# Tensor sums moved from GpSimd to VectorE, attention of two head groups in one operation: an attention and FFN kernel

## Chip, core and metric

The kernel runs on one core of one Trainium2 chip. The time is that of the device from launch to end, in microseconds. Of a kernel the median of several runs is given; one more execution, with the profiler on, gave the trace. TensorE is called PE in the profile (PEld is its weight load), VectorE DVE, ScalarE ACT, GpSimd POOL, SyncE SP.

## What is computed

```python
def _attn_ref(q, k, v):                     # 8 batches, 8 heads, 576 tokens, 64 columns
    chunk, scale = 64, 1.0 / np.sqrt(D)     # attention inside chunks of 64 tokens
    scores = scale * np.matmul(q_c, k_c.transpose(0, 1, 2, 4, 3))
    scores = scores - np.max(scores, axis=-1, keepdims=True)
    attn = np.exp(scores)
    attn = attn / (np.sum(attn, axis=-1, keepdims=True) + 1e-09)
    return np.matmul(attn, v_c)

def _moe_ref(x, w_in, w_out):               # x 4608 x 512, w_in 512 x 2048, w_out 2048 x 512
    h = x @ w_in
    g = np.where(h >= 1, h, np.where(h <= -1, 0.0, (h + 1) ** 2 / 4.0))
    return (g @ w_out).astype(np.float32)
```

x is the attention's result with the heads side by side. The weights come in 64-bit floats, q, k and v in 32-bit ones.

## The kernel before

**Tiles.** The 4608 tokens are nine tiles of 512: tiles 0 to 5, 7 and 8 are the first 512 tokens of a batch, tile 6 collects the last 64 of all eight. A tile has four head groups of two heads each (128 columns of x). In SBUF x stands with its columns on the partitions, so FFN1 gives h by blocks of 128 hidden columns by 512 tokens.

**Products.** Each 32-bit operand is split into a high part that PE takes in its fast 32-bit format and a low part, the rest; a product is high x high + high x low + low x high, three matmuls of 512 columns. The high part is a copy on ScalarE, the low part a subtraction on VectorE (`ffn_split` L760, `split` L1050, `parts` L946, `attn_split_banks` L723).

**Tiles 0 to 2** are done one by one: `ffn_in` makes a block of h (L739), the curve (ScalarE L746, L749; VectorE L750) makes g, `ffn_split` its parts, `ffn_out` (L774) adds the block's share to four banks of PSUM. At the tile's end `store` (L792 on VectorE, L794 on ScalarE) moves the banks into two buffers and SP sends them out. Meanwhile `mix_weights` makes, for 16 pairs of weight blocks, the sums that a seven-product scheme for 2 x 2 blocks needs: per call two sums of 512 columns on GpSimd and four of 256 columns on VectorE (L837), ScalarE's copies (L859), VectorE's low parts (L860), and DMAs from GpSimd into a DRAM tensor `mixed` (L823). SCHEDULE (L262) says at which block (tile x 16 + block) each call is added, and which buffers it uses.

**Tiles 3 to 8** are done in three pairs with seven products in place of eight. `mix_x` (L937, L944, L946) makes the combinations of x. For FFN1, `ffn_quad(t, m)` does seven products n of 1.36 us each for two blocks of hidden columns of two tiles, in the order SEQ = (1, 5, 6, 3, 7, 2, 4), into two banks (ps_h for even m, ps_o for odd m), with sums of what stands in the banks (L975, L981) and the curve (L1008 to L1012). Four quads make a half. Then `ffn_mixed_out` takes the half's 28 steps of FFN2: `split` (ScalarE L1049, VectorE L1050) and the products, with `less` (L985) making the next combinations of g. The weights of both come back from `mixed` by GpSimd's DMAs (L887, 512 KB for two products), into a ring of seven buffers; `stream(done)` asks for the next ones. The results are transposed on VectorE and sent by SP (`store_turned`, L1089, L1110, L1118).

**Attention** of the next tiles goes beside the FFN, for tiles 2 and up in bursts of two head groups: values of the current two groups (L568) and scores of the next two (L550) on PE, then for each group by itself max, subtraction, exp, sum, reciprocal and product (`attn_softmax`, L626 to L644), a transpose in 32 x 32 blocks (L675), and eight SP transfers for both groups (`move`, L668) that put the blocks in place. q and k are transposed the same way (`attn_turn`, L524). The product by the reciprocal is on GpSimd for tiles 0, 2, 3 and 4.

**Order.** Nothing is emitted directly. Every step goes to a `Plan` with an engine, a cost, what it reads and writes, and a lag from its end to its use (a DMA's landing). The plan is run twice in the kernel's build: once in the order of the program, from which due times are worked out backwards, then engine by engine, always the step that is ready and has the earliest due time. That order becomes each engine's queue, which runs in order on the chip. Steps of the kind "any" (`less` L985, the subtractions of `mix_x` L937) go to VectorE or GpSimd, whichever takes them first in the plan. `port=True` marks steps that the plan doesn't let overlap on the two engines:

```python
            if port:
                start = max(start, port_free)
            end = self.products_end(start, cost, columns) if e == "pe" else start + cost
            if port:
                port_free = end
```

Of the kernel before, what the change touches and what calls it, by code (L numbers as in the profile page):

```python
# [211 lines left out]
def kernel(  # L212
# [15 lines left out]
    nc = tc.nc  # L228
# [27 lines left out]
    PAIRED = 3  # L256
# [4 lines left out]
    OWN, RING5, EARLIER, LATER = range(4)  # L261
# [10 lines left out]
    def buffers(pool, name, n, dtype=F32):  # L272
# [73 lines left out]
    def e_room(t, g):  # L346
        return room("e", kT_bufs if t > 1 else e_bufs, t, g)
# [139 lines left out]
    def load_heads(t, g, which="qkv"):  # L487
        for n, src, bufs in (("q", q, q_bufs), ("k", k, k_bufs), ("v", v, v_bufs)):
# [5 lines left out]
            if BATCH[t] is None or (n, t) == ("v", TURNED):  # L494
# [6 lines left out]
                (), (key,), lag=2.1 if t < 3 else 4.1, moving=1.3 if load == load_blocks else 1.2,  # L501
# [15 lines left out]
    def attn_turn(t, g):  # L517
        for n, (name, bufs, src_bufs, dst_bufs) in enumerate(
# [38 lines left out]
    def values_of(t, g):  # L557
# [6 lines left out]
        def product(n, h, half):  # L564
            at = (2 * n + h) * C if t < FLIPPED else h * HALF + n * C
            of = h * HALF + n * C
            rows = slice(half * C, (half + 1) * C)
            nc.tensor.matmul(  # L568
                out=values[half][h * C:(h + 1) * C, n * C:(n + 1) * C],
                lhsT=v_sb[rows, of:of + C], rhs=aT[rows, at:at + C], start=True, stop=True,  # L570
            )
# [43 lines left out]
    def attn_softmax(t, g):  # L615
# [5 lines left out]
        e4 = e.rearrange("p (n h k) -> p h n k" if t < FLIPPED else "p (h n k) -> p h n k", h=2, k=C)  # L621
        mx4 = mx.rearrange("p (h n) x -> p h n x", h=2)
        sm4 = sm.rearrange("p (n h) x -> p h n x" if t < FLIPPED else "p (h n) x -> p h n x", h=2)
# [18 lines left out]
        on_pool = t < 1 or t in (2, 3, 4)  # L642
# [15 lines left out]
    def attn_turn_back_pair(some):  # L658


        xkeys, akeys = ([f"{n}{i}" for i in range(2)] for n in ("qT", "aT"))

        def move():
            src, dst = (x.rearrange("p g (c e q) -> p (g c) e q", e=2, q=Q) for x in (qT_both, aT_both))
# [7 lines left out]
        for t, g in some:  # L672
            ekey, e = e_room(t, g)
            xkey, x = room("x", qT_bufs, t, g)
            plan.add("dve", 0.6, lambda x=x, e=e: nc.vector.transpose(out=x, in_=e), (ekey,), (xkey,))  # L675
        plan.add("sp", 5.4, move, xkeys, akeys, lag=4.9, moving=0.8, sends=8)
# [127 lines left out]

    def step_of(w, m, n):
# [11 lines left out]
    def to_mixed(w, m, which, key, src, cols, after):  # L817
# [5 lines left out]
        plan.add("pool", 0.65, lambda: nc.gpsimd.dma_start(  # L823
            out=mixed[steps[0] // LONG][:, rows, cols], in_=src()
        ), key, [f"mixed{step}_{cols.start}" for step in steps], lag=2.1, moving=0.8, after=after)

    def mix_weights(kind, m, scratch, after):
# [44 lines left out]
    def engine_of(e):  # L872
        return nc.vector if e == "dve" else nc.gpsimd

    RING = [f"wi{j}" for j in range(6)] + ["wo0"]
    X_TAGS = [f"wi{j}" for j in range(6, NF)]
    asked_for = [0]

    def stream(done):


        while asked_for[0] < min(len(RING) + done // 2, (NTILE - PAIRED) // 2 * STEPS // 2):
            step, tag = asked_for[0] * 2 % STEPS, RING[asked_for[0] % len(RING)]
            asked_for[0] += 1
            keys = [f"mixed{n}_{at}" for n in (step, step + 1)
                    for at in ((0,) if product_of[n] in SINGLE else (0, HALF))]
            plan.add("pool", 0.65, lambda step=step, tag=tag: nc.gpsimd.dma_start(  # L887
                out=place_of(tag).bitcast(F32), in_=mixed[step // LONG][:, step % LONG:step % LONG + 2, :]
            ), keys, (f"{tag}_0", f"{tag}_1"), lag=2.1, moving=1.4)

    def streamed(t, w, m, n):


        step = (t - PAIRED) // 2 * STEPS + step_of(w, m, n)
        tag, at = RING[step // 2 % len(RING)], step % 2
        return f"{tag}_{at}", lambda: place_of(tag)[:, at, :]
# [28 lines left out]
    def mix_x(t):  # L925
# [63 lines left out]
    def ffn_quad(t, m):  # L989


        abank, bbank = h_banks if m % 2 == 0 else o_banks[:2]
        s_, w_, u_ = H_SUMS[m % 2]
        k = m % PARTS
# [11 lines left out]
        def curve(src, dst):  # L1006
            (hkey, h), (rkey, r) = src, dst
            plan.add("act", 0.5, lambda: nc.scalar.activation(  # L1008
                out=r(), in_=h(), func=AF.Relu, bias=0.5, scale=0.5
            ), (hkey,), (rkey,))  # L1010
            plan.add("act", 0.52, lambda: nc.scalar.square(out=r(), in_=r()), (), (rkey,))  # L1011
            plan.add("dve", 0.6, lambda: nc.vector.scalar_tensor_tensor(  # L1012
                out=r(), in0=h(), scalar=1.0, in1=r(), op0=ALU.max, op1=ALU.min
            ), (hkey,), (rkey,))
# [9 lines left out]
        curve(u_, X12[k])  # L1024
        products(7, bbank, False)
        total_of(w_, bbank, w_)
        curve(w_, X22[k])
        products(2, abank, True)
        total_of(s_, abank, s_)
        curve(s_, X11[k])  # L1030
        products(4, bbank, False)
        curve(whole(bbank), X21[k])
# [9 lines left out]
    def ffn_mixed_out(t, half, at):  # L1042
# [14 lines left out]
        for index, n in enumerate(SEQ):  # L1057
# [24 lines left out]
            done = (t - PAIRED) // 2 * STEPS + step_of("wo", half * PARTS + PARTS - 1, n) + 1  # L1082
            stream(done)

    def store_turned(t, n, src, ending=False):
# [3 lines left out]
        plan.add("dve", 0.6, lambda: nc.vector.transpose(out=o(), in_=x()), (key,), (okey,))  # L1089
# [30 lines left out]
        plan.add("sp", 0.6 * sends, send, (okey,), (), lag=2.3, moving=0.9, sends=sends)  # L1120
# [48 lines left out]
    def scratch_of(where):  # L1169
# [5 lines left out]
        if where == OWN:  # L1175
            return [S_BUFS[n] for n in (0, 3, 4, 0)]
        if where == EARLIER:
# [176 lines left out]
```

## Time and profile before

| | us |
|---|---|
| median of 3 runs (lowest, highest) | 854.37 (853.62, 856.25) |
| the profiled execution's own time | 856.74 |
| its span, first to last instruction | 855.0 |
| PE busy | 807.4 |
| DVE busy | 713.7 |
| ACT busy | 494.1 |
| POOL busy (DMA issues among it) | 359.9 |

Busy is the time in which at least one instruction of the engine was under way. Matmuls are pipelined, one starts before the last ends. The span's stages, by the trace: to 120 us attention of the first tiles, tile 0 and the preparation of the weights; to 236 tile 1; to 365 tile 2; to 530, 700 and 845 the three pairs; then the last store.

### The profile page before, as it was taken

The page shows a single profiled execution, that of the slowest core. Times are in us where ns is not written, and L with a number is a line of the kernel's source. Part 1 is how long each engine was busy: PE and PEld are TensorE (multiplying, and loading weights), DVE is VectorE, ACT ScalarE, POOL GpSimd, SP SyncE. Part 2 cuts the span into 40 slices and gives each one's busy share as a digit, 9 for nine tenths or more (in the row PEclk, how much of TensorE's full clock was granted, in tenths as well). Part 3 has the DMA queues.
Part 4 walks back from the last instruction along what each step waited for, and adds up shares of the span by engine and source line. Part 5 has one row for each costly group of instructions (what it writes and reads, how often), then busy time and mean ns, then how long its engine had stood idle before and what let it go on. Part 6 is the DMA issues. An engine that isn't in the chain of part 4 may idle for free.

```text
span 855.0 us, 15680 instructions
## 1 busy us (share of the span) xinstructions
PE 807.4 (94%) x5648; PEld 655.4 (77%) x5648; DVE 713.7 (83%) x1092; ACT 494.1 (58%) x870; POOL 359.9 (42%) x419
## 2 busy tenths in 40 slices
PE   9999999989989989999998799899998999999995
PEld 8888878877768868878886578778786877788873
DVE  4989986989669888999797899798589986866795
ACT  5999844534426444765476436564477456637741
POOL 1000015886656681464526353254138532631351
PEclk9999999999999999999999999999999999999998
DMA  9995758796799795998998469999774599566654
GB/s 201 279 314 112 204 113 228 221 291 190 217 214 304 177 277 123 271 243 226 262 261 210 141 184 217 224 242 262 204 203 142 168 265 250 177 193 189 191 168 79
DMA packets 334350, 180.38 MB, mean 211 GB/s; under 512 B 293824, under 2 KB 302016, under 8 KB 334272
## 3 DMA queue, kind: packets, MB, share of 16 engines
q0 software_dynamic: 33152, 117.46, 42.7%
q1 hardware_dynamic: 296896, 61.12, 35.6%
q10 hardware_dynamic: 4224, 0.79, 0.6%
q8 instruction: 45, 0.74, 0.4%
q14 instruction: 33, 0.27, 0.1%
HBM read 133.17 MB, written 38.80 MB: 201 GB/s over the span
## 4 chain that ended last, share of the span: by engine, by line
PE 49%; DVE 20%; DMA 11%; SPq 6%; issue 5%; POOL 4%; ACT 3%; DVEq 0%; POOLq 0%; ACTq 0%
PE ps_o L966 22%; PE ps_h L739 8%; PE ps_o L774 7%; PE ps_h L966 7%; DMA out_dram<-tmp 3%; DVE big_wo L1050 3%; DMA k_sb<-in_k_dram 2%; POOL mixed L823 2%; DVE gl L1050 2%; DVE big_wo L1012 2%; DMA aT_both<-qT_both 1%; PE ps_h L1314 1%; DVE big_wo L975 1%; DVE big_wi L946 1%; SPq L470 1%
## 5 line engine op out<-in xcount | busy, mean ns | idle before, releaser
L887 POOL DMA_DIRECT2D big_wi<-mixed x144 | 78.2, 544 | 198.3 <-PE ps_o L966 132.0
L739 PE MATMUL ps_h<-xh,parts_wi 128*128 128x512 f32 x376 | 128.5, 402 | 8.3 <-DVE r L750 4.4
L774 PE MATMUL ps_o<-parts_wo,gh 128*128 128x512 f32 x384 | 120.5, 395 | 4.4 <-DVE tmp L792 4.4
L966 PE MATMUL ps_o<-big_wo,big_wi 128*128 128x512 f32 x432 | 107.8, 393 | 3.6 <-DVE big_wo L1050 3.4
L966 PE MATMUL ps_o<-gh,big_wi 128*128 128x512 f32 x288 | 98.7, 396 | 7.6 <-DVE big_wo L1012 5.4
L966 PEld LDWEIGHTS ps_o<-big_wo,big_wi 128*128 128x128 f32 x432 | 80.7, 189 | 23.1 <-DVE big_wo L1050 6.4
L985 POOL TENSOR_TENSOR big_wo<-big_wo,big_wo 128x512 f32<-128x512 f32 x55 | 85.9, 1571 | 25.7 <-DVE gl L1050 15.0
L739 PEld LDWEIGHTS ps_h<-xh,parts_wi 128*128 128x128 f32 x376 | 72.6, 193 | 25.6 <-DVE r L750 5.6
L966 PE MATMUL ps_o<-big_wi,big_wi 128*128 128x512 f32 x360 | 88.1, 396 | 0.2 <-ACT big_wo L981 0.2
L966 PE MATMUL ps_h<-big_wi,big_wi 128*128 128x512 f32 x360 | 86.6, 391 | 0.0
L774 PEld LDWEIGHTS ps_o<-parts_wo,gh 128*128 128x128 f32 x384 | 71.3, 189 | 19.9 <-DVE tmp L792 5.2
L1050 DVE TENSOR_TENSOR big_wo<-big_wo,big_wo 128x512 fp32r<-128x512 f32 x84 | 79.1, 950 | 4.0 <-ACT big_wo L1049 4.0
L1049 ACT CAST big_wo<-big_wo 128x512 fp32r<-128x512 f32 x84 | 52.0, 622 | 51.9 <-PE ps_o L966 28.5
L966 PEld LDWEIGHTS ps_o<-big_wi,big_wi 128*128 128x128 f32 x360 | 67.3, 189 | 16.4 <-ACT big_wo L981 1.9
L966 PEld LDWEIGHTS ps_h<-big_wi,big_wi 128*128 128x128 f32 x360 | 68.0, 189 | 14.8 <-ACT r L981 0.5
L1050 DVE TENSOR_TENSOR gl<-big_wo,gh 128x512 fp32r<-128x512 f32 x84 | 77.3, 927 | 2.2 <-ACT gh L1049 2.0
L774 PE MATMUL ps_o<-parts_wo,gl 128*128 128x512 f32 x192 | 75.6, 394 | 0.2 <-issue 0.2
L739 PE MATMUL ps_h<-xl,parts_wi 128*128 128x512 f32 x188 | 75.0, 399 | 0.0
L1049 ACT CAST gh<-big_wo 128x512 fp32r<-128x512 f32 x84 | 52.0, 621 | 38.0 <-PE ps_o L966 32.4
L966 PEld LDWEIGHTS ps_o<-gh,big_wi 128*128 128x128 f32 x288 | 54.6, 190 | 22.2 <-DVE big_wo L1012 7.0
L975 DVE TENSOR_TENSOR big_wo<-ps_o,big_wo 128x512 f32<-128x512 f32 x84 | 55.7, 677 | 6.4 <-PE ps_o L966 6.3
L1011 ACT ACTIVATE big_wo<-big_wo 128x512 f32<-128x512 f32 x96 | 59.4, 630 | 1.9
(205 smaller groups left out, 1669.7 us busy)
## 6 DMA issues: line engine op xcount, KB each, us to landing
big_wi<-mixed POOLq DMA_DIRECT2D x144, 512.0 KB, 4.9
big_wo<-mixed POOLq DMA_DIRECT2D x24, 512.0 KB, 4.5
mixed<-tmp POOLq DMA_DIRECT2D x36, 256.0 KB, 4.3
words_wi<-in_moe_w_in_dram SPq DMA_DIRECT2D x16, 512.0 KB, 6.3
words_wo<-in_moe_w_out_dram SPq DMA_DIRECT2D x16, 512.0 KB, 6.7
aT_both<-qT_both SPq DMA_DIRECT2D x112, 64.0 KB, 3.8
v_sb<-in_v_dram SPq DMA_DIRECT2D x52, 128.0 KB, 4.2
q_sb<-in_q_dram SPq DMA_DIRECT2D x104, 64.0 KB, 4.3
```

The source lines that it names most:

```text
L470: queue.dma_start(out=dst[r:r + Q, :, e, :], in_=rows[:, e * Q:(e + 1) * Q, :].rearrange("c p d -> p c d"),)
L739: nc.tensor.matmul(out=ps, lhsT=weight["wi", j][:, half, kc * P:(kc + 1) * P], rhs=x(), start=(kc == 0 and i == 0), stop=(kc == KC - 1 and ...
L774: nc.tensor.matmul(out=acc, lhsT=x[:, cols], rhs=weight["wo", j][:, half, :], start=(j == 0 and i == 0), stop=(j == NF - 1 and i == 2),)
L823: plan.add("pool", 0.65, lambda: nc.gpsimd.dma_start(out=mixed[steps[0] // LONG][:, rows, cols], in_=src()), key, [f"mixed{step}_{cols.sta ...
L887: plan.add("pool", 0.65, lambda step=step, tag=tag: nc.gpsimd.dma_start(out=place_of(tag).bitcast(F32), in_=mixed[step // LONG][:, step % ...
L966: nc.tensor.matmul(out=bank, lhsT=w[:, part * HALF + c * P:part * HALF + (c + 1) * P], rhs=rhs, start=fresh and begin and k == 0, stop=end ...
L975: plan.add("dve", 0.6, lambda: nc.vector.tensor_tensor(out=o(), in0=b, in1=x(), op=ALU.add), (bkey, xkey), (okey,))
L985: plan.add("any", (0.6, 1.1), lambda e: engine_of(e).tensor_tensor(out=o(), in0=x(), in1=y(), op=ALU.subtract), (xkey, ykey), (okey,), por ...
L1011: plan.add("act", 0.52, lambda: nc.scalar.square(out=r(), in_=r()), (), (rkey,))
L1012: plan.add("dve", 0.6, lambda: nc.vector.scalar_tensor_tensor(out=r(), in0=h(), scalar=1.0, in1=r(), op0=ALU.max, op1=ALU.min), (hkey,), ( ...
L1049: plan.add("act", 0.52, lambda: nc.scalar.copy(out=h(), in_=x()), (key,), (hkey,))
L1050: plan.add("dve", 0.6, lambda: nc.vector.tensor_tensor(out=l(), in0=x(), in1=h().bitcast(F32), op=ALU.subtract), (key, hkey), (lkey,), por ...
```

## The change

1. The two wide sums of `mix_weights`, the subtractions of `mix_x` and all of `less` are VectorE's. GpSimd keeps DMA issues and the softmax product of tile 0.
2. From tile 2 on, attention's operations on VectorE and ScalarE take both groups of a burst at once: q, k and their transposes, the softmax and its transpose are 128 x 1024. For that the buffers of two groups are one tile (`twin`). The transposed result is first copied whole on ScalarE; then four SP transfers instead of eight put the off-diagonal blocks in place.
3. FFN1's products of neighbouring quads are interleaved in the program and in the stream's order: quad m + 1 begins after four products of quad m (PACE = 2). `stream` is called after each product instead of after each quad.
4. The plan's lags: transfers into and out of `mixed` 3.3 instead of 2.1 us, turned stores 3.3 instead of 2.3, loads of q, k, v for tile 2 4.1 instead of 2.1. Some costs in the plan are changed by a few hundredths.
5. SCHEDULE has other places and buffers for the 16 calls of `mix_weights`; the last is at 44 instead of 47.

New functions for one more way of doing tiles (`ffn_quad_held`, `recall`) are added and not called, since MIXED equals PAIRED. The diff, cut:

```diff
-    PAIRED = 3
+    PAIRED, MIXED, PACE = 3, 3, 2
...
     SCHEDULE = (
-        (17, RING5), (18, EARLIER), (18, EARLIER), (20, RING5), (22, RING5), (23, EARLIER),
-        (25, RING5), (27, RING5), (31, RING5), (34, RING5), (35, LATER), (37, RING5),
-        (37, RING5), (42, RING5), (43, OWN), (47, OWN),
+        (17, EARLIER), (18, RING5), (20, EARLIER), (20, EARLIER), (20, RING5), (22, RING5),
+        (27, RING5), (31, RING5), (32, RING5), (34, LATER), (37, RING5), (37, RING5),
+        (38, RING5), (39, OWN), (43, OWN), (44, OWN),
     )
...
-                (), (key,), lag=2.1 if t < 3 else 4.1, moving=1.3 if load == load_blocks else 1.2,
+                (), (key,), lag=2.1 if t < 2 else 4.1, moving=1.3 if load == load_blocks else 1.2,
...
+    def attn_turn_pair():
+        for src, dst in (("q_sb", "qT"), ("k_sb", "kT")):
+            plan.add("dve", 1.18, lambda src=src, dst=dst: nc.vector.transpose(
+                out=flat[dst], in_=flat[src]
+            ), [f"{src}{i}" for i in range(2)], [f"{dst}{i}" for i in range(2)])
...
-        on_pool = t < 1 or t in (2, 3, 4)
+        on_pool = t < 1
...
-    def attn_turn_back_pair(some):
+    def attn_softmax_pair():
+        keys = {n: [f"{n}{i}" for i in range(2)] for n in ("ps_a", "mx", "sm", "kT", "qT", "aT")}
+        sc = a_pair.rearrange("p h (m k) -> p (h m) k", k=C)
+        e3 = flat["kT"].rearrange("p (m k) -> p m k", k=C)
+        plan.add("dve", 1.13, lambda: nc.vector.tensor_reduce(
+            out=mx_both, in_=sc, axis=AX.X, op=ALU.max
+        ), keys["ps_a"], keys["mx"])
+        plan.add("dve", 1.13, lambda: nc.vector.tensor_tensor(
+            out=e3, in0=sc, in1=mx_both.broadcast_to([P, 2 * G, C]), op=ALU.subtract
+        ), (*keys["ps_a"], *keys["mx"]), keys["kT"])
+        plan.add("act", 0.9, lambda: nc.scalar.activation(
+            out=flat["kT"], in_=flat["kT"], func=AF.Exp, scale=SCALE
+        ), (), keys["kT"])
+        def norm():
+            nc.vector.tensor_reduce(out=sm_both, in_=e3, axis=AX.X, op=ALU.add)
+            nc.vector.tensor_scalar_add(sm_both, sm_both, 1e-9)
+            nc.vector.reciprocal(out=sm_both, in_=sm_both)
+        plan.add("dve", 1.6, norm, keys["kT"], keys["sm"])
+        plan.add("dve", 1.13, lambda: nc.vector.tensor_tensor(
+            out=e3, in0=e3, in1=sm_both.broadcast_to([P, 2 * G, C]), op=ALU.mult
+        ), keys["sm"], keys["kT"], port=True)
         def move():
...
             for j in range(2):
-                for i in range(4):
-                    a, b = ((2 * j + n) * Q for n in divmod(i, 2))
-                    nc.sync.dma_start(
-                        out=dst[b:b + Q, :, i // 2, :], in_=src[a:a + Q, :, i % 2, :]
-                    )
...
-        plan.add("sp", 5.4, move, xkeys, akeys, lag=4.9, moving=0.8, sends=8)
+                for n in range(2):
+                    a, b = (2 * j + n) * Q, (2 * j + 1 - n) * Q
+                    nc.sync.dma_start(out=dst[b:b + Q, :, n, :], in_=src[a:a + Q, :, 1 - n, :])
+        plan.add("dve", 1.18, lambda: nc.vector.transpose(out=flat["qT"], in_=flat["kT"]), keys["kT"], keys["qT"])
+        plan.add("act", 0.9, lambda: nc.scalar.copy(out=flat["aT"], in_=flat["qT"]), keys["qT"], keys["aT"])
+        plan.add("sp", 2.7, move, keys["qT"], keys["aT"], lag=4.9, moving=0.4, sends=4)
...
+    QUAD_ORDER = sorted(
+        ((m, n) for m in range(PARTS) for n in SEQ), key=lambda x: (len(SEQ) * x[0] + PACE * SEQ.index(x[1]), x[0])
+    )
+    OUT_ORDER = [(k, n) for n in SEQ for k in range(PARTS)]
...
-        at = k * len(SEQ) + SEQ.index(n) if w == "wi" else SEQ.index(n) * PARTS + k
+        at = (QUAD_ORDER if w == "wi" else OUT_ORDER).index((k, n))
...
-    STEPS = NF * len(SEQ)
+    STEPS, SLACK = NF * len(SEQ), 1.2
...
-        ), key, [f"mixed{step}_{cols.start}" for step in steps], lag=2.1, moving=0.8, after=after)
+        ), key, [f"mixed{step}_{cols.start}" for step in steps], lag=2.1 + SLACK, moving=0.8, after=after)
...
-            plan.add("pool" if wide else "dve", 1.1 if wide else 0.35, lambda: (nc.gpsimd if wide else nc.vector).tensor_tensor(
+            plan.add("dve", 0.6 if wide else 0.35, lambda: nc.vector.tensor_tensor(
...
-                plan.add("any", (0.6, 1.1), lambda e, i=i: engine_of(e).tensor_tensor(
+                plan.add("dve", 0.6, lambda i=i: nc.vector.tensor_tensor(
                     out=o()[:, i, :], in0=x()[:, i, :], in1=y()[:, i, :], op=ALU.subtract
...
-        plan.add("any", (0.6, 1.1), lambda e: engine_of(e).tensor_tensor(
+        plan.add("dve", 0.6, lambda: nc.vector.tensor_tensor(
             out=o(), in0=x(), in1=y(), op=ALU.subtract
...
-        plan.add("sp", 0.6 * sends, send, (okey,), (), lag=2.3, moving=0.9, sends=sends)
+        plan.add("sp", 0.55 * sends, send, (okey,), (), lag=3.3, moving=0.9, sends=sends)
...
-            for m in range(half * PARTS, (half + 1) * PARTS):
-                if m == 0:
-                    out_until(t * NF - 1)
-                ffn_quad(t, m)
-                stream((t - PAIRED) // 2 * STEPS + step_of("wi", m, SEQ[-1]) + 1)
-                if m in QUAD_BURSTS and more:
+            quads = [ffn_quad(t, half * PARTS + k) for k in range(PARTS)]
+            for part, n in QUAD_ORDER:
+                m = half * PARTS + part
+                quads[part](n)
+                stream(position(t, "wi", m, n) + 1)
+                if n == SEQ[-1] and m in QUAD_BURSTS and more:
```

## Rows read from the trace of the kernel before

**Rows 1.** Page: busy us (share of the span) and instructions.

```profile
PE 807.4 (94%) x5648; PEld 655.4 (77%) x5648; DVE 713.7 (83%) x1092; ACT 494.1 (58%) x870; POOL 359.9 (42%) x419
```

**Rows 2.** Table by stage: length; busy PE, PEld, DVE, ACT, POOL (count); clock; DMA; GB/s.

```profile
120.00:236.00 116.00, 110.54 (x854) 90.40 (x845) 94.43 (x159) 52.21 (x90) 80.43 (x92) 0.99 0.78 220
236.00:365.00 129.00, 121.59 (x989) 98.41 (x987) 108.61 (x173) 66.03 (x118) 72.26 (x85) 0.97 0.87 229
365.00:530.00 165.00, 154.08 (x1123) 122.85 (x1122) 148.86 (x214) 95.84 (x168) 76.36 (x88) 0.99 0.83 218
530.00:700.00 170.00, 161.84 (x985) 130.72 (x984) 145.11 (x211) 99.65 (x175) 73.59 (x84) 0.98 0.82 213
700.00:845.00 145.00, 141.61 (x614) 114.03 (x612) 112.87 (x148) 81.00 (x138) 52.37 (x63) 1.00 0.67 187
```

**Rows 3.** Waits of PE by releaser: total us, times, longest.

```profile
PE ps_o L966 <- DVE big_wo L1050: 5.5, 3, 2.1
PE ps_o L966 <- DVE big_wo L1012: 5.4, 3, 2.0
PE ps_o L774 <- DVE tmp L792: 4.4, 2, 3.1
PE ps_h L739 <- DVE r L750: 4.4, 2, 4.1
PE ps_h L739 <- DVE xl L723: 3.9, 1, 3.9
```

**Rows 4.** Timeline: DVE, GpSimd (POOL) and PE: start us, us, instruction.

```profile
183.17 1.77 DVE L760 TENSOR_TENSOR gl<-r,gh 128x512 fp32r<-128x512 f32 x1
...
186.66 1.44 DVE L837 TENSOR_TENSOR tmp<-tmp 128x256 f32<-128x256 f32 x1
...
310.65 1.28 DVE L629 TENSOR_TENSOR kT<-ps_a,mx 128x512 f32<-128x512 f32 x2
311.85 5.17 DVE L937 TENSOR_TENSOR big_xl<-big_xl,big_xl 128x512 f32<-128x512 f32 x1
...
311.43 2.55 POOL L937 TENSOR_TENSOR big_xh<-big_xl,big_xh 128x512 f32<-128x512 f32 x2
313.94 1.29 POOL L937 TENSOR_TENSOR big_xl<-big_xl,big_xl 128x512 f32<-128x512 f32 x1
315.18 1.27 POOL L837 TENSOR_TENSOR e<-parts_wo 128x512 f32<-128x512 f32 x1
...
320.01 0.50 PE L739 MATMUL ps_h<-xh,parts_wi 128*128 128x512 f32 x1 [4.13 <-DVE r L750]
```

**Rows 5.** Groups by line, DVE: busy us, mean ns | idle before.

```profile
L414 DVE TENSOR_TENSOR parts_wi<-tmp,parts_wi 128x512 fp32r<-128x512 f32 x16 | 10.9, 683 | 0.8 <-ACT parts_wi L410 0.4
...
L837 DVE TENSOR_TENSOR tmp<-e 128x256 f32<-128x256 f32 x4 | 1.7, 418 | 1.1 <-DMA out_dram<-tmp 1.1
```

**Rows 6.** Busy DVE (and POOL): L1050, L760, L1012, L946, L985, L937, L837 in turn.

```profile
0.00:855.00 855.00, 153.73 (x168) 0.99 0.79 211
...
0.00:855.00 855.00, 42.39 (x48) 0.99 0.79 211
...
0.00:855.00 855.00, 71.44 (x96) 0.99 0.79 211
...
0.00:855.00 855.00, 33.28 (x42) 0.99 0.79 211
...
0.00:855.00 855.00, 26.27 (x31) 100.56 (x65) 0.99 0.79 211
...
0.00:855.00 855.00, 9.24 (x4) 28.59 (x20) 0.99 0.79 211
...
0.00:855.00 855.00, 32.93 (x64) 43.47 (x32) 0.99 0.79 211
```

**Rows 7.** Waits of DVE for transfers: total us, times, longest.

```profile
DVE qT_both L524 <- DMA k_sb<-in_k_dram: 5.7, 2, 4.7
...
DVE tmp L792 <- DMA out_dram<-tmp: 5.0, 1, 5.0
```

More of the change, by code (lines that the diff above doesn't have):

```diff
@@ L569, in product @@
                 out=values[half][h * C:(h + 1) * C, n * C:(n + 1) * C],
-                lhsT=v_sb[rows, of:of + C], rhs=aT[rows, at:at + C], start=True, stop=True,
+                lhsT=v_sb[rows, of:of + C], rhs=(aT if t < FLIPPED else flat["aT"])[rows, at:at + C],
+                start=True, stop=True,
             )
@@ L870, in mix_weights @@
             ], slice(0, T), after)
-    def engine_of(e):
-        return nc.vector if e == "dve" else nc.gpsimd
-    RING = [f"wi{j}" for j in range(6)] + ["wo0"]
+    RINGS = [f"wi{j}" for j in range(4)], [f"wi{j}" for j in range(6)] + ["wo0"]
     X_TAGS = [f"wi{j}" for j in range(6, NF)]
     asked_for = [0]
-    def stream(done):
-        while asked_for[0] < min(len(RING) + done // 2, (NTILE - PAIRED) // 2 * STEPS // 2):
-            step, tag = asked_for[0] * 2 % STEPS, RING[asked_for[0] % len(RING)]
-            asked_for[0] += 1
[L885 to L889, printed above, removed]
+    ALONE = NF // 2 * len(SEQ) * (MIXED - PAIRED) // 2
@@ new lines, with position, steps_at, slot_of @@
+    held_steps = [step_of("wi", m, n) for m in range(NF // 2) for n in SEQ]
+    def position(t, w, m, n):
+        step = step_of(w, m, n)
+        return held_steps.index(step) if t < MIXED else ALONE + (t - MIXED) // 2 * STEPS + step
+    def steps_at(at):
+        at -= at % 2
+        if at < ALONE:
+            return sorted(held_steps[at:at + 2])
+        return [(at - ALONE) % STEPS + n for n in range(2)]
+    def slot_of(at):
+        ring = RINGS[at >= ALONE]
+        return ring[(at - ALONE * (at >= ALONE)) // 2 % len(ring)]
@@ new lines, in stream @@
+    def stream(done, without=0):
+        while asked_for[0] * 2 < ALONE + (NTILE - MIXED) // 2 * STEPS:
+            at = asked_for[0] * 2
+            late = at >= ALONE
+            begun = done - ALONE * late
+            if begun < 0 or at - ALONE * late >= 2 * (len(RINGS[late]) - without + begun // 2):
+                return
+            asked_for[0] += 1
+            steps, tag = steps_at(at), slot_of(at)
+            keys = [f"mixed{n}_{part}" for n in steps
+                    for part in ((0,) if product_of[n] in SINGLE else (0, HALF))]
+            first, last = (step % LONG for step in steps)
+            plan.add("pool", 0.65, lambda n=steps[0] // LONG, rows=slice(first, last + 1, last - first), tag=tag: (
+                nc.gpsimd.dma_start(out=place_of(tag).bitcast(F32), in_=mixed[n][:, rows, :])
+            ), keys, (f"{tag}_0", f"{tag}_1"), lag=2.1 + SLACK, moving=1.4)
@@ L1004, in products, with curve, ffn_quad_held, hold @@
             plan.add("pe", 1.362, emit, (skey, *hkeys, *lkeys), (key,), columns=6 * T)
[L1006 to L1014, printed above, removed]
+        return products
+    def curve(src, dst):
+        (hkey, h), (rkey, r) = src, dst
+        plan.add("act", 0.5, lambda: nc.scalar.activation(
+            out=r(), in_=h(), func=AF.Relu, bias=0.5, scale=0.5
+        ), (hkey,), (rkey,))
+        plan.add("act", 0.52, lambda: nc.scalar.square(out=r(), in_=r()), (), (rkey,))
+        plan.add("dve", 0.6, lambda: nc.vector.scalar_tensor_tensor(
+            out=r(), in0=h(), scalar=1.0, in1=r(), op0=ALU.max, op1=ALU.min
+        ), (hkey,), (rkey,))
+    def ffn_quad_held(t, m):
+        i, j = 2 * m, 2 * m + 1
+        abank, bbank = h_banks if m % 2 == 0 else h_banks[::-1]
+        s_, w_, u_ = HELD_SUMS
+        products = first_product(t, m)
+        def hold(j, r):
+            rkey, r = r
+            plan.add("pool", 0.65, lambda: nc.gpsimd.dma_start(out=held[j], in_=r()), (rkey,),
+                     (f"held{j}",), lag=2.1 + SLACK, moving=0.8)
         products(1, bbank, True)
@@ L1176, in scratch_of @@
             return [S_BUFS[n] for n in (0, 3, 4, 0)]
+        if where == SPARE:
+            return [(f"wi4_{n}", lambda n=n: place_of("wi4")[:, n, :].bitcast(F32)) for n in range(2)] + S_BUFS[3:]
         if where == EARLIER:
@@ L1244, in attention @@
                 if j + 2 in BURSTS:
-                    for at in then:
-                        attn_turn(*at)
+                    if m + 1 < 2 * NP:
+                        attn_turn(*then[0])
+                    else:
+                        attn_turn_pair()
                 elif m + 1 < 2 * NP:
@@ L1272 @@
             ffn_split(t, j)
-            for n, own, what in MIX_AT:
-                if n == t * NF + j:
-                    mix_weights(*what, scratch_of(own), len(plan.parts) - 1)
+            mixes_at(t * NF + j)
     stream(0)
```

123 lines of the change are left out of this document (79 added, 44 removed).

## The prediction

> **What bounds the kernel now.** I read the busy line first: PE is busy 807.4 of 855.0 us, DVE 713.7, and GpSimd does tensor work beside its DMA issues [rows 1]. The table by stage [rows 2] says where PE loses time, in two ways: idle, and at a granted clock below full. Idle is the stage's length less PE busy: 5.5 us in 120 to 236, 7.4 in 236 to 365, 10.9 in 365 to 530, 8.2 in 530 to 700, 3.4 in 700 to 845, together 35.4. The granted clock of these stages is 0.99, 0.97, 0.99, 0.98 and 1.00; (1 - clock) times length is 1.2 + 3.9 + 1.7 + 3.4 + 0 = 10.2 us, time lost to stretches at 1.2 instead of 2.4 GHz. So 45.6 us are to be had in all. The first 120 us and the end behind 845 stay out of the count: the change hardly touches them.
>
> The waits of PE say who is late: DVE ends the five costliest, 23.6 us [rows 3]. So the question is why DVE is late, though it is less busy than PE.
>
> The timeline of 310 to 320 shows it [rows 4]. Two operations that read PSUM (L629) take 1.28 us, one every 0.60. Then a 512-column subtraction, L937, starts at 311.85 and takes 5.17 us; from 311.43 on GpSimd runs four such operations back to back. PE stops for 4.13 us, for the r that stands behind L937 in DVE's queue. L760 at 183.17, with 1.77 us, and L837 at 186.66, with 1.44, are the same on a small scale; they stand in the queue ahead of the L723 that ends a 3.9 us stall [rows 3, 4]. Undisturbed, an operation of that shape takes 683 ns (L414) [rows 5]. Sums over lines say how much that is in all [rows 5, 6]: L1050 takes 153.73 us for 168 operations instead of 168 x 0.683 = 114.7, so 39.0 too many; in the same way L760 9.6, L1012 5.9, L946 4.6, L985 5.1, L937 6.5, and L837 against 418 ns for 256 columns 6.2. Together 77 us of DVE's 713.7 are spent waiting beside GpSimd.
>
> The Trainium skill, SBUF — State Buffer, Who interferes with whom, says that the port pair which both engines share is an exclusive lock, held for one instruction by whoever issues first. By that rule L937 would have stood behind one GpSimd operation, taken about 2.0 us, and the forecast gain would be some 3 us smaller. The trace shows it behind four, and decides.
>
> **The change, part by part.**
>
> *GpSimd's sums to VectorE.* 65 (L985), 20 (L937) and 32 (L837) operations leave GpSimd [rows 6]. On DVE each adds the 0.60 us of L629 [rows 4], so 117 x 0.60 = 70 us, on an engine that PE waits for. Against them stand the 77 us. DVE's load hardly changes; what goes are single operations of 1.5 to 5 us in front of what PE waits for. GpSimd keeps its DMA issues, which no longer queue behind sums, and the products of tile 0's softmax, inside the first 120 us.
>
> *Attention of two groups at once.* For 14 pairs (tiles 2 to 8) max, subtraction, sum, product and three transposes become 1024-column operations. From 418 ns at 256 columns and 683 at 512, another 512 add about 0.53 us [rows 5]; one wide operation takes 1.13 from start to start where two took 1.20. Seven of them save 0.5 us a pair, one scalar add and one reciprocal less perhaps 0.3: 0.8 x 14 = 11 us less on DVE. The 12 products of tiles 2 to 4 that come from GpSimd add 6 x 1.13 = 7. Net 4 less. But what PE needs can now stand behind 1.2 us instead of 0.7. No row shows a 1024-column f32 operation. Bounds: a gain of 4, if DVE's time were PE's, and a loss of 0.5 on PE in each of 14 pairs, 7 us. I take a loss of 4, towards that end, since PE's stalls are waits for single operations [rows 3].
>
> *Turning back.* A 1024-column ScalarE copy per pair (an estimate of 1.1 us, DVE's wide one) is new and stands ahead of 4 transfers on SP in place of 8. What it hides behind: ScalarE is 58% busy [rows 1], and the values product that needs the tile comes a burst later. I cost it at nothing; uncovered it would be 14 x 1.1 = 15 us, and a gain of as much if four fewer issues were on the path.
>
> *FFN1 products of neighbouring quads interleaved.* The same products and banks in another order, which the ring of seven stream buffers follows. The planner orders by due time and may mix quads already, so this part may do nothing at all. Bounds: the 5.4 us of L1012, FFN1's curve [rows 3], as a gain, and the same as a loss if a ring buffer is held for two quads. I take nothing, the middle.
>
> *Longer lead.* The planner counts 1.2 us more for weights through DRAM, 1.0 for turned stores, 2.0 for the loads of tile 2. Issues move ahead on GpSimd's and SP's queues past others; no byte is added. DVE stood 5.0 us for a store's landing, which PE feels at L792, 4.4, and 5.7 for k [rows 3, 7]. Bounds: those 10.7 won; or 4.7, the longest wait for k, lost where a load moved ahead crowds another. Half is taken, inside the stage sums.
>
> *Sums of weights at other places* (from 17 to 44 instead of 17 to 47). Two of them, at 31 and 32, now stand just ahead of tile 1's store, and share buffers with it: one wait like L792's, 4.4 us, more or less. I take nothing.
>
> **The sum, by stage.** From 120 to 365: the 4.1 at L750 go, and of the 3.9 at L723 what the two operations ahead of it took too long, 1.77 - 0.68 and 1.44 - 0.42, 2.1. With L792's these are the three long stalls, so I give a third of the 5.1 us of clock to each, 3.4 to these two. Of L792's 4.4 and 1.7, half: 3.0. That makes 12.6. From 365 to 700: 19.1 us idle and 5.1 of clock, in which DVE's contention and late transfers are mixed; half, 12, and no more, since DVE stays busy there (148.86 of 165 and 145.11 of 170 us) [rows 2]. From 700 to 845 half of 3.4, 1.7. Less 4 for the wide operations: 22.3 us. The profiled execution took 856.74 around its span of 855.0, and would take 834; the median of the three runs is 854.37, and 854.4 - 22.3 = 832.
>
> **Rivals.**
>
> *DVE's queue is the bound from 365 to 700.* The operations that GpSimd did stand in the same in-order queue as everything else. For it: DVE's busy share there, 90 and 85%. Against: much of that is the waiting that goes. Then only the 12.6 of 120 to 365 are won: 842.
>
> *Nearly all of it goes.* DVE's times become regular, the planner's order holds, PE doesn't stop and keeps its clock: 854.4 - 45.6 is 809, and 812 with a few short waits left. Against: transfers end some of the waits.
>
> *The stalls move.* What was late has successors that were late too (the seven-buffer ring, the two store buffers), and a wait of the same size takes the place of each: 853.
>
> *Wide operations hold up PE, and it is slower.* A wide transpose starts when q and k of both groups have landed; DVE stands still until then, as it did for 4.7 us for one k [rows 7], and everything behind it waits. It decides once each of the 14 pairs loses PE more than 26.3 / 14 = 1.9 us, 26.3 being the gain above without the wide operations' 4. At 3 us each, 42 - 26 = 16 over before: 870. Against: there are two such waits in 855 us so far, and before, the scores of both groups were one step as well. The Trainium skill, Perfetto Trace Analysis, Optimizing Scalar/DVE Operations, says that where VectorE isn't saturated but causes bubbles on other engines, breaking instructions up may complete work sooner. By it this part goes the wrong way; with DVE 83% busy and at the end of PE's waits, the trace of before meets its condition.
>
> *The change doesn't do what it says*: that is the interleaving, above, costed at nothing.
>
> **How the numbers follow.** The forecast has a chance of 0.50, DVE's queue 0.22, nearly all 0.09, stalls that move 0.07, the wide operations 0.12. Faster by over 0.3% (2.6 us, about what a measurement of this kernel can tell from no change) is below 851.8: the first three and a little of the fourth, 0.82; within it 0.06; slower 0.12. The range goes down to 812, nearly all of it; and up to 849, the first rival with 7 us lost to the wide operations. Outside are the last two cases, under 0.2.
>
> **What would show it.** L1050 near 683 ns in the mean, and no DVE operation of 512 columns over 1 us behind 120: the contention is gone. PE idle in the two stages of tiles 1 and 2 at 6 us or less in place of 12.9, at a clock of 0.99 or more: the first term is right. DVE above 95% busy from 365 to 700 and PE's waits still at L1050 and L1012: the first rival. DVE's waits for q and k above 20 us: the slower one. The forecast is wrong in its root if L1050 falls to 683 and PE's idle time does not fall.

## The result, and the profile after

The changed kernel takes 825.12 us (median of 4 runs, 824.52 to 825.72) where the kernel before took 854.11 on the same chip: a ratio of 0.9656, interval 0.9638 to 0.9674, 29 us less. In later sessions the kernel before took 842 to 858, so what follows goes by ratios of one session and by the traces.

The page's busy line of the changed kernel, to be read against [rows 1]:

```profile
PE 794.4 (96%) x5648; PEld 652.5 (79%) x5648; DVE 684.1 (83%) x1095; ACT 501.3 (61%) x870; POOL 176.1 (21%) x290
```

The span went from 855.0 to 823.6 us. PE is busy 13.0 us less with the same 5648 matmuls, and idle 18.4 us less (47.6 to 29.2). So some 40% of the gain came out of time that the page calls busy. Of the 13.0 us, 3.4 are the granted clock: ahead of the last store 20.5 us stood at 1.2 GHz before, 13.7 now, and half the difference is lost time. Another 6.9 are short stalls that the overlapping records cover: at 2.4 GHz most 512-column matmuls start 227 ns behind the one before, and 139 starts were more than 260 ns behind in the kernel before, 86 now. DVE takes 117 sums over from GpSimd, and is busy 30 us less.

The costliest groups on DVE, against [rows 5, 6] (L1050 is now L1159, L985 is L1038, L760 is L786):

```profile
L1159 DVE TENSOR_TENSOR gl<-big_wo,gh 128x512 fp32r<-128x512 f32 x84 | 56.8, 681 | 8.8 <-ACT gh L1158 8.8
L1159 DVE TENSOR_TENSOR big_wo<-big_wo,big_wo 128x512 fp32r<-128x512 f32 x84 | 56.8, 682 | 5.9 <-ACT big_wo L1158 5.7
L1038 DVE TENSOR_TENSOR big_wo<-big_wo,big_wo 128x512 f32<-128x512 f32 x72 | 48.2, 682 | 0.2
L786 DVE TENSOR_TENSOR gl<-r,gh 128x512 fp32r<-128x512 f32 x48 | 32.8, 683 | 7.8 <-ACT gh L785 7.4
...
L673 DVE TENSOR_REDUCE mx_both<-ps_a 128x16 f32<-128x1024 f32 x14 | 17.1, 1219 | 5.0 <-PE ps_a L558 5.0
```

Every mean is at the undisturbed 683 ns; the 77 us of waiting beside GpSimd are gone. The wide operations take 1.22 us, as the extrapolation had it.

The waits of PE, against [rows 3]:

```profile
PE ps_h L765 <- ACT big_xh L729: 6.0, 1, 6.0
PE ps_o L1019 <- DVE big_wo L1159: 5.7, 1, 5.7
PE ps_o L1019 <- DVE big_wo L1066: 2.6, 2, 2.1
```

Two stalls are left that matter, at 246 and 553 us. Both end at a store. Here are SP, DVE, ACT and PE at the first (timeline; SPq are SP's DMA issues):

```profile
222.92 5.79 SPq L826 DMA_DIRECT2D out_dram<-tmp  x3
229.47 2.89 SPq L698 DMA_DIRECT2D aT_both<-qT_both  x4
232.47 14.15 SPq L466 DMA_DIRECT2D k_sb_both<-in_k_dram  x8
246.66 0.49 SPq L826 DMA_DIRECT2D out_dram<-tmp  x1
...
249.03 0.43 DVE L868 TENSOR_TENSOR tmp<-tmp,e 128x256 f32<-128x256 f32 x1 [7.11 <-DMA out_dram<-tmp]
...
250.75 0.62 ACT L890 CAST tmp<-tmp 128x512 fp32r<-128x512 f32 x1 [9.55 <-DVE e L868]
251.27 0.58 ACT L729 COPY big_xh<-ps_h 128x512 f32<-128x512 f32 x1
...
251.90 0.79 PE L765 MATMUL ps_h<-xh,parts_wi 128*128 128x512 f32 x1 [5.95 <-ACT big_xh L729]
```

The last piece of tile 1's store stands on SP's queue behind four moves and eight loads of k. A sum of weights on DVE wants the store's buffer, a cast on ACT wants the sum, and the copy that frees PE's bank stands behind the cast. At 553 it is the transpose of a turned store:

```profile
557.78 0.71 DVE L1197 STREAM_TRANSPOSE tmp<-big_wo 128x512 f32<-128x512 f32 x1 [7.73 <-DMA out_dram<-tmp]
```

**By stage.** The boundaries below are counted, not read off the clock: tiles 1 and 2 begin with the 193rd and 385th of the 576 FFN1 matmuls (L739, now L765), the three pairs with the 1st, 673rd and 1345th of the 2016 of L966 (now L1019), and the rest begins with the last of them. So tile 2 begins at 217.7 us of the kernel before and the pairs at 332.6, 511.5 and 686.5, and not at the 236, 365, 530 and 700 that are given for them ahead of the prediction. Each row is one trace, in us; the other kernels are explained below. Two traces of the same kernel (after and n1, e5 and n2) differ by up to 2.4 us in a stage.

```
kernel                start   tile 1  tile 2  pair 1  pair 2  pair 3   rest    span
before                123.2    94.5   114.9   178.9   175.0   158.2   10.3    855.0
after                 122.1    88.1   111.9   164.5   173.1   154.6    9.2    823.6
e1 sums alone         124.7    88.1   116.9   170.4   166.9   156.6    9.3    832.9
e2 sums back          122.7    88.1   108.8   179.5   175.7   161.0    9.2    845.2
e7 idle sums          124.1    93.7   110.6   186.8   187.8   173.4    9.2    885.7
e8 idle fills         123.2    90.6   109.9   165.8   170.0   155.5    9.3    824.2
e4 short lead         122.0    88.3   110.6   163.3   172.0   155.6    9.2    821.0
e6 old places         122.6    88.1   117.4   164.9   170.1   154.8    9.3    827.2
e3 quads in turn      122.9    88.4   110.9   166.0   173.0   154.8    9.3    825.4
e5 narrow             122.3    88.2   102.7   168.5   167.6   154.7    9.2    813.1
n1 after again        122.2    88.1   111.3   164.5   170.7   155.0    9.2    821.0
n2 narrow again       122.4    88.2   102.3   168.6   167.1   156.2    9.3    814.0
n3 eight transfers    121.4    88.2   114.0   178.3   166.9   154.0    9.2    832.0
n4 narrow in turn     121.7    88.1   102.3   169.7   168.2   153.8    9.3    813.0
```

### The profile page after: what moved, and what is told of

It is laid out like the page before. It is cut to its first block, busy times and chain, and to the rows that moved or that the text cites. A ratio compares the mean times of both kernels' runs of the same rounds, so it can differ in the third digit from the quotient of the medians.

```text
span 823.6 us, 15371 instructions
## 1 busy us (share of the span) xinstructions
PE 794.4 (96%) x5648; PEld 652.5 (79%) x5648; DVE 684.1 (83%) x1095; ACT 501.3 (61%) x870; POOL 176.1 (21%) x290
## 4 chain that ended last, share of the span: by engine, by line
PE 68%; DVE 12%; DMA 6%; ACT 5%; issue 5%; SPq 3%; POOL 1%; DVEq 0%; ACTq 0%; POOLq 0%
PE ps_o L1019 30%; PE ps_h L765 12%; PE ps_o L800 12%; PE ps_h L1019 8%; DMA out_dram<-tmp 3%; SPq L466 2%; DVE big_wo L1066 1%; ACT big_wo L1062 1%; PE ps_a L558 1%; DVE gl L1159 1%; DVE big_wo L1159 1%; DVE big_wo L1038 1%; ACT big_wo L1065 1%; POOL mixed L854 1%; DMA k_sb_both<-in_k_dram 1%
## 5 line engine op out<-in xcount | busy, mean ns | idle before, releaser
L765 PE MATMUL ps_h<-xh,parts_wi 128*128 128x512 f32 x376 | 127.6, 399 | 6.0 <-ACT big_xh L729 6.0
L1019 PE MATMUL ps_o<-big_wo,big_wi 128*128 128x512 f32 x432 | 107.3, 393 | 5.7 <-DVE big_wo L1159 5.7
L1019 PE MATMUL ps_o<-gh,big_wi 128*128 128x512 f32 x288 | 98.1, 395 | 3.2 <-DVE big_wo L1066 2.1
L1019 PEld LDWEIGHTS ps_o<-big_wo,big_wi 128*128 128x128 f32 x432 | 81.3, 189 | 23.5 <-DVE big_wo L1159 6.5
L765 PEld LDWEIGHTS ps_h<-xh,parts_wi 128*128 128x128 f32 x376 | 71.8, 191 | 21.8 <-ACT big_xh L729 6.4
L1019 PE MATMUL ps_o<-big_wi,big_wi 128*128 128x512 f32 x324 | 81.0, 392 | 0.9 <-DVE big_wo L1066 0.5
L1019 PE MATMUL ps_h<-big_wi,big_wi 128*128 128x512 f32 x324 | 79.4, 391 | 1.1 <-DVE big_wo L1066 1.1
L765 PE MATMUL ps_h<-xl,parts_wi 128*128 128x512 f32 x188 | 74.2, 394 | 0.0
L1019 PEld LDWEIGHTS ps_o<-big_wi,big_wi 128*128 128x128 f32 x324 | 60.3, 188 | 15.5 <-ACT tmp L1034 1.7
L1019 PEld LDWEIGHTS ps_h<-big_wi,big_wi 128*128 128x128 f32 x324 | 60.3, 188 | 14.6 <-DVE big_wo L1066 1.7
L1019 PEld LDWEIGHTS ps_o<-gh,big_wi 128*128 128x128 f32 x288 | 54.9, 191 | 15.9 <-DVE big_wo L1066 2.5
L1159 DVE TENSOR_TENSOR gl<-big_wo,gh 128x512 fp32r<-128x512 f32 x84 | 56.8, 681 | 8.8 <-ACT gh L1158 8.8
L1159 DVE TENSOR_TENSOR big_wo<-big_wo,big_wo 128x512 fp32r<-128x512 f32 x84 | 56.8, 682 | 5.9 <-ACT big_wo L1158 5.7
L1019 PE MATMUL ps_o<-gl,big_wi 128*128 128x512 f32 x144 | 56.9, 395 | 0.3 <-DVE gl L1159 0.3
```

What stands on the lines that cost most here:

```text
L765: nc.tensor.matmul(out=ps, lhsT=weight["wi", j][:, half, kc * P:(kc + 1) * P], rhs=x(), start=(kc == 0 and i == 0), stop=(kc == KC - 1 and ...
L1019: nc.tensor.matmul(out=bank, lhsT=w[:, part * HALF + c * P:part * HALF + (c + 1) * P], rhs=rhs, start=fresh and begin and k == 0, stop=end ...
L1159: plan.add("dve", 0.6, lambda: nc.vector.tensor_tensor(out=l(), in0=x(), in1=h().bitcast(F32), op=ALU.subtract), (key, hkey), (lkey,), por ...
```

## Experiments

Theories: A, GpSimd's sums held up VectorE's and so PE. B, the gain comes from the lead, the places or the order of products. C, VectorE's queue is the bound. D, GpSimd's results and DMA issues came late, and its neighbourhood as such cost nothing. E, SP's queue became shorter.

**e1, the sums alone**, on the kernel before (cut; the subtractions of `mix_x` are changed as `less` is):

```diff
-            plan.add("pool" if wide else "dve", 1.1 if wide else 0.35, ...
+            plan.add("dve", 0.6 if wide else 0.35, ...
...
-        plan.add("any", (0.6, 1.1), lambda e: engine_of(e).tensor_tensor(
+        plan.add("dve", 0.6, lambda: nc.vector.tensor_tensor(
...
-        on_pool = t < 1 or t in (2, 3, 4)
+        on_pool = t < 1
```

> The kernel before with only the first part: all sums and the softmax products of tiles 2 to 4 on VectorE. Theory A (GpSimd's sums held up VectorE's, and that made PE wait): L1050 falls from 950 and 927 ns to about 683, and most of the 29 us come: 828 to 842. Theory B (the gain is from the lead, the places and the order of products): L1050 falls, but the time stays at 848 to 856. Theory C (VectorE's queue takes the sums' time from PE): above 856.

836.38 us against 848.0, ratio 0.9833 (0.977 to 0.9896). L1050 is at 683 and 684 ns, where [rows 6] gives 915 in the mean. That is A, but with about half of the gain and not most of it. B's range is missed, C is out.

**e2, the sums back**, the other way round: the three places of e1 undone in the changed kernel, except for attention's product.

> The changed kernel with the sums where they were before: wide sums of the weights on GpSimd, subtractions on either engine. Theory A: 843 to 856, and L1159 well above 683 ns. Theory B: 824 to 832.

849.06 against 848.0, ratio 0.9998 (0.9961 to 1.0036): all other parts together give nothing as long as GpSimd adds. Its L1162 (the same operation):

```profile
L1162 DVE TENSOR_TENSOR big_wo<-big_wo,big_wo 128x512 fp32r<-128x512 f32 x84 | 82.9, 995 | 3.8 <-ACT big_wo L1161 3.6
L1162 DVE TENSOR_TENSOR gl<-big_wo,gh 128x512 fp32r<-128x512 f32 x84 | 79.7, 960 | 6.8 <-ACT gh L1161 6.6
```

The table places the loss: against n1 the span is 24.2 us longer, the three pairs, where `less` is, 26.0 longer, and tile 2 is 2.5 shorter.

**e7, idle sums, and e8, idle fills**: GpSimd works beside 113 of the moved sums (226 additions or 565 fills in the traces; 116 were meant) on a tile that nobody reads, so no engine waits for its data, and VectorE's, ScalarE's and PE's queues are those of the changed kernel. The comments in the cut say what e8 has in place of a line.

```diff
+    def pool_work(share, of):
+        seen[0] += 1
+        if seen[0] % of < share:
+            for _ in range(2):                      # e8: range(5)
+                nc.gpsimd.tensor_tensor(out=idle, in0=idle, in1=idle, op=ALU.add)   # e8: nc.gpsimd.memset(idle, 0.0)
```

> The changed kernel with GpSimd adding a 304-column tile of its own to itself, twice beside each of 116 of the sums; nobody reads it and the plan doesn't know of it, so the queues of the other engines are the same. Theory A: VectorE's operations with operands in SBUF get longer (means of 800 to 950 ns at L1159), PE waits for VectorE, 835 to 855. Theory D (what cost time before was the wait for GpSimd's results and its late DMA issues, not the neighbourhood): 824 to 830.

> The same at the same places, but five fills of that tile, which read nothing and take GpSimd about as long (1.6 us by the MEMSET rows). If reading beside VectorE is what counts, L1159 stays at 683 ns and the time at 824 to 830; if any work of GpSimd, or the DMA issues behind it, as the run with idle sums.

The groups of GpSimd's work and of DVE's L1159 (L1179 here), e7:

```profile
L359 POOL TENSOR_TENSOR idle<-idle 128x304 f32<-128x304 f32 x226 | 204.7, 906 | 12.3
...
L1179 DVE TENSOR_TENSOR gl<-big_wo,gh 128x512 fp32r<-128x512 f32 x84 | 75.0, 898 | 10.3 <-ACT gh L1178 10.3
L1179 DVE TENSOR_TENSOR big_wo<-big_wo,big_wo 128x512 fp32r<-128x512 f32 x84 | 70.5, 844 | 6.2 <-ACT big_wo L1178 6.2
...
L1045 DVE TENSOR_TENSOR big_wo<-ps_o,big_wo 128x512 f32<-128x512 f32 x84 | 56.2, 677 | 2.3 <-PE ps_o L1036 1.8 <-ACT big_wo L1051 0.5
```

and e8:

```profile
L359 POOL MEMSET idle<- 128x304 f32 x565 | 201.3, 356 | 27.1
...
L1179 DVE TENSOR_TENSOR gl<-big_wo,gh 128x512 fp32r<-128x512 f32 x84 | 57.2, 685 | 9.4 <-ACT gh L1178 9.2
L1179 DVE TENSOR_TENSOR big_wo<-big_wo,big_wo 128x512 fp32r<-128x512 f32 x84 | 57.2, 686 | 7.8 <-ACT big_wo L1178 7.7
```

With 204.7 us of idle sums the kernel takes 883.13, ratio 1.0377 (1.0295 to 1.0459), slower than before and above what A expected. With 201.3 us of fills, which keep GpSimd as busy (1.78 us at each place against 1.81), L1179 stays at 685 ns and the trace's span is 824.2, that of the changed kernel; the timed median is 831.67, ratio 0.9789 (0.9712 to 0.9866), a little above the 824 to 830 expected.

Both kernels have something in them besides GpSimd's work: most of PE's 512-column matmuls start 231 ns apart where the changed kernel and e1 have 227 (medians), and they do so from 32 to 115 us already, where GpSimd does no idle work. By the means, 230.4 and 227.2 ns, that is 3.2 ns times some 3060, about 10 us. It comes with the idle tile, and no run shows why. So some 10 of e7's 62 us are not the sums', and e8's one per cent above the changed kernel is about what these matmuls cost. Its trace has the changed kernel's span because PE is idle less, 20.7 us in place of 29.2.

What counts is GpSimd reading SBUF while VectorE has both operands there: in e7 L1045, with one operand in PSUM, stays at 677 ns beside the same sums, and L710's transposes, with one operand, at 1237. The Trainium skill, SBUF — State Buffer, Who interferes with whom, names just this pair of cases, two SBUF inputs against a GpSimd operation that reads SBUF, and the two runs agree. D falls as far as it is about late DMA issues: with the fills they stand behind as much work of GpSimd, and no time of its own shows. That GpSimd's results came late isn't ruled out as a part of what e1 won: in the kernel before ScalarE waited 16.8 us for sums of GpSimd's (L985 and L937), PE never directly, and no run separates this wait from VectorE's longer operations.

**e4, short lead**, the three lags of before (SLACK 0, stores 2.3, tile 2's loads 2.1; with the store's the plan's old cost of 0.6 us an issue):

> The changed kernel with the plan's lags of before (2.1 us for the transfers through DRAM, 2.3 for turned stores, 2.1 for the loads of tile 2). If the lead hid transfers: 828 to 838, with more waits of VectorE for transfers than now. If it does nothing: 822 to 828.

823.47 against 849.66, ratio 0.9663 (0.9603 to 0.9724), the changed kernel's own. VectorE waits more for transfers, 30.9 us against 25.2, but the time doesn't show it: the lead does nothing that can be told within 5 us.

**e6, old places**, SCHEDULE of before in the changed kernel:

> The changed kernel with the places and buffers of the weights' sums of before. Prediction: nothing, give or take one wait of 4.4 us: 821 to 830. The 6 us stall near 246 us stands behind a sum at place 32 that waits for the buffer of tile 1's store; with the old places (31 and 34) it should be gone or shorter, and if nothing replaces it the time is 818 to 821.

829.13, ratio 0.9727 (0.9657 to 0.9797). My guess was wrong: PE still stops at tile 1's store, now for ScalarE's part of it (L820), 9.7 us in two waits, and tile 2 takes 117.4 us in place of 111.9. By the ratios the new places are worth 3 to 6 us, with an interval of 6 either way.

**e3, quads in turn**, PACE = 1:

> The changed kernel with FFN1's quads in turn again (PACE = 1), all else as changed. Prediction's value for the interleaving: nothing, 822 to 828. If it was worth the 5.4 us of L1012 of before: 828 to 832, with waits of PE at L1066.

828.4, ratio 0.9719 (0.965 to 0.9788), not clear of the changed kernel's. n4 below repeats it.

**e5, narrow**: each wide operation as two of 512 columns, by halves that have a key of their own, with the same layout and the same four moves.

```diff
+        for h in range(2):
+            half, ms = slice(h * T, (h + 1) * T), slice(h * G, (h + 1) * G)
+            kT, mx, sm = flat["kT"][:, half], mx_both[:, ms, :], sm_both[:, ms, :]
...
+            plan.add("dve", 0.6, lambda s3=s3, mx=mx: nc.vector.tensor_reduce(
+                out=mx, in_=s3, axis=AX.X, op=ALU.max
+            ), (f"ps_a{h}",), (f"mx{h}",))
...
```

> The changed kernel with each 1024-column operation of attention on VectorE and ScalarE as two of 512, each waiting for its own half alone; layout and transfers as changed. If wide operations hold up what PE needs (prediction: 4 us lost): 819 to 823. If their 11 us less of VectorE time counts: 829 to 836. Otherwise 823 to 828.

815.77 against 849.66, ratio 0.957 (0.9507 to 0.9634): the fastest so far. Four kernels beside each other then settled what was in it.

**n1**, the changed kernel; **n2**, e5's kernel; **n3**, n2 with eight moves and no copy on ScalarE; **n4**, n2 with PACE = 1. The diff of n3 against n2, cut:

```diff
-                for n in range(2):
-                    a, b = (2 * j + n) * Q, (2 * j + 1 - n) * Q
-                    nc.sync.dma_start(out=dst[b:b + Q, :, n, :], in_=src[a:a + Q, :, 1 - n, :])
+                for i in range(4):
+                    a, b = ((2 * j + n) * Q for n in divmod(i, 2))
+                    nc.sync.dma_start(out=dst[b:b + Q, :, i // 2, :], in_=src[a:a + Q, :, i % 2, :])
...
-            plan.add("act", 0.48, lambda x=x, aT=aT: nc.scalar.copy(out=aT, in_=x), (f"qT{h}",), (f"aT{h}",))
-        plan.add("sp", 2.7, move, keys["qT"], keys["aT"], lag=4.9, moving=0.4, sends=4)
+        plan.add("sp", 5.4, move, keys["qT"], keys["aT"], lag=4.9, moving=0.8, sends=8)
```

> The changed kernel, as it is, beside the three below. 822 to 828.

> The kernel with attention's operations in halves again, beside the changed one on the same chip. If the wide operations cost time by where PE's work stands behind them: 8 to 11 us under the changed kernel. If the first result was the chip's: within 3 us of it.

> The narrow kernel with the turned tile moved by eight transfers, as before the change, and no ScalarE copy. Theory E (four transfers fewer per pair shorten SP's queue, in which stores and loads of k wait): 4 to 12 us over the narrow kernel, and more waits of VectorE for transfers. Prediction (nothing): within 3 us of it.

> The narrow kernel with FFN1's quads in turn. If the interleaving is worth something by itself: 3 to 6 us over the narrow kernel, as the run in turn suggested of the changed one. Prediction (nothing): within 3 us.

Against 847.89 of before: n1 822.85, ratio 0.9691 (0.9659 to 0.9724); n2 815.35, 0.9588 (0.9551 to 0.9625); n3 832.41, 0.9799 (0.9763 to 0.9836); n4 813.21, 0.9564 (0.9525 to 0.9602).

*n4*: interleaving quads is worth nothing. *n2*: narrow is 7.5 us faster than the changed kernel, again, a little less than the 8 to 11 expected. But the table says where: 9.0 us in tile 2; of the pairs, 4.1 slower, 3.6 faster, 1.2 slower. So it isn't the width that PE feels at every burst. It is the one stall of 246 us, which none of the three traces of a narrow kernel with four moves has, and the clock behind it. In n1 the stall is 5.3 us, and the granted clock from 236 to 320 us is 0.96, where n2's is 1.00 (length; busy PE, PEld, DVE, ACT, POOL; clock; DMA; GB/s; n1, then n2):

```profile
236.00:320.00 84.00, 77.96 (x684) 63.87 (x683) 67.28 (x102) 42.39 (x71) 28.57 (x40) 0.96 0.79 217
```

```profile
236.00:320.00 84.00, 83.86 (x723) 68.96 (x723) 77.15 (x145) 47.98 (x84) 32.39 (x46) 1.00 0.86 235
```

The clock is worth 84 x 0.04 = 3.4 us; with the stall that makes 8.7 of the 9.0. *n3*: four more moves per pair cost 17 us, more than the 4 to 12 expected: 11.7 in tile 2 and 9.7 in pair 1, with 2.2 back in pair 3. E holds. SP's queue at tile 1's store, n3:

```profile
227.58 7.75 SPq L704 DMA_DIRECT2D aT_both<-qT_both  x8
235.43 1.04 SPq L835 DMA_DIRECT2D out_dram<-tmp  x2
...
240.33 0.59 ACT L829 COPY tmp<-ps_o 128x512 f32<-128x512 f32 x1 [10.22 <-DMA out_dram<-tmp]
...
240.97 1.22 PE L809 MATMUL ps_o<-parts_wo,gh 128*128 128x512 f32 x2 [6.45 <-ACT tmp L829]
```

and n2:

```profile
225.63 0.36 SPq L834 DMA_DIRECT2D out_dram<-tmp  x1
227.62 1.98 SPq L466 DMA_DIRECT2D k_sb_both<-in_k_dram  x4
229.69 0.43 SPq L834 DMA_DIRECT2D out_dram<-tmp  x1
230.22 4.29 SPq L704 DMA_DIRECT2D aT_both<-qT_both  x4
```

In n3 two pieces of the store are issued only behind eight moves, 7.75 us, and PE stops 6.45 for the buffer; in n2 they are out before the four moves begin. q's transpose writes the tile that the moves read, and DVE waits for them, here over the whole trace, n3 and then n2:

```profile
DVE qT_both L545 <- DMA aT_both<-qT_both: 12.9, 6, 4.1
```

```profile
DVE qT_both L545 <- DMA aT_both<-qT_both: 2.8, 2, 1.5
```

In pair 1 these waits are 6.6 us in n3 and none in n2. That they make up the 9.7 us there is likely, not shown.

## Why the prediction was right, and where it was wrong

The time was forecast at 832 with a range of 812 to 849, and came out at 825.1. The mechanism held: GpSimd's sums beside VectorE's were the brake (e1, e2, e7). That the time came so near is in part luck, as the terms of the sum show:

*GpSimd's sums to VectorE.* As forecast: L1050 at 682 ns, no disturbed operation. Behind 120 us no DVE operation of 512 columns takes over 0.8 us. DVE is busy 684, where 703 follows from 77 less, 70 more, 4 less; 18 of the other 19 us lie in this term, by which DVE's busy time was to stay where it was: with the sums and the products alone, in e1, it is 695.7.

*From 120 to 365, 12.6; from 365 to 700, 12; from 700, 1.7.* The stages are bounded here by the FFN matmul that comes next at each of these times in the kernel before; to the same matmuls of the changed kernel the gains are 9.2, 16.6 and 3.5 us, 29.3 in all. In the first stage the L723 and L750 stalls are gone. The half of L792 that was counted is not: the stall at tile 1's store grew from 4.4 us in two waits to 6.0 in one and changed its name, because a transfer ends it. PE is idle 7.2 us there, not the 6 or less that was named as the sign.

The terms were taken from PE's idle time and clock, 45.6 us, as all there was to be had, and 26.3 of it were to be won. In the three stages idle time fell by 16.9 us and the clock gave back 3.4, 20.3 in all: less than forecast. The other 9.0 came out of PE's busy time, which the prediction put at nothing; most of it is the short stalls told above. This more than made up for the 6 us that were missing. With the 4 us taken off for the wide operations, which these stages don't show, the time came out 7 below the forecast.

*Attention at once, a loss of 4.* Not seen as such. n2 is 7.5 us faster than n1, near the bound of 7, but by one stall of another kind and its clock; the pairs, where 7 of the 14 wide bursts stand, are 1.7 us apart in sum and the other way. The slower rival falls with it: DVE's waits for q and k are 1.5 us, where it wanted above 20. The 11 us less on DVE came (695.7 in e1, 684.1 here).

*Turning back, nothing.* This is the step that failed. I asked whether the ScalarE copy is covered and not what four issues per pair do to the queue that they leave. At 0.7 to 0.8 us an issue on SP in the mean, with stores, k and q behind them, four moves in place of eight, the copy with them, are worth 17 us in the narrow kernel (n3); in the changed kernel itself this wasn't measured. The bound of 15 us that stood beside it was near by luck: it is the copy's time, 14 x 1.1, and no time of an issue.

*Longer lead, half of 10.7.* Wrong: e4 has none of the lead and the same time. Nor were the waits won that the term counted on. DVE's waits for transfers are 25.0 us before and 25.2 after: those for k, q and the moves fell from 9.4 to 3.0, those for stores grew from 14.0 to 20.7.

*Interleaving, nothing*: right (n4). *Places, nothing, 4.4 either way*: not settled (e6).

*The rivals.* DVE's queue as the bound falls: pair 1 alone gave 14 us at 145.50 busy of 160 (320 to 480 us), and from 365 to 700 DVE is 87% busy (290.81 of 335), not above 95. Stalls that move: one did, at tile 1's store, and it cost what n2 saves. How the parts add up is seen in part, by ratios of different sessions: 0.983 for the sums alone (e1), 0.980 with all the rest but four moves and wide operations (n3), 0.959 with the four moves (n2), 0.969 with the wide operations too (n1). e1 and n3, both with eight moves, stop PE at the same store, for 7.8 us in two waits and 6.4 in one. What doesn't fit is e2: four moves and wide operations, by these about 1% together, give nothing there. That the moves' delay is hidden behind GpSimd's as long as that lasts would explain it; no run shows it.

The narrow kernel, n2 or n4, beats both: 813 to 815 us, ratio 0.956 to 0.959.

## What to carry to other kernels

Before giving GpSimd elementwise work on SBUF, look at the duration of VectorE's operations beside it: the cost stands there, in rows of an engine that does something else. When transfers are taken off a queue, price what stands behind them on that queue, not only the operation that replaces them. And a PE that is 94% busy may hide stalls in the busy time: count the time of a stage against the number of its matmuls.

## What was not expected of the hardware

A GpSimd addition of 304 columns took 906 ns beside VectorE, a fill of the same tile 356; with 226 such additions VectorE was busy 86 us more (769.9 against 684.1) and the span 62 us longer, some 10 of them by PE's slower matmuls, and still more than the sums of the kernel before cost. That a tile of 304 columns which only GpSimd touches comes with matmuls 231 ns apart in place of 227 has no explanation here. A single VectorE operation can stand behind several GpSimd operations in a row: 5.17 us in [rows 4].
